# Attention loop: where the bursts of row maxima and their transposition stand among the matmuls

## The chip, the cores and the metric

The kernel runs on one core of a Trainium2 chip. The metric is device time in microseconds (us) of one execution; less is better. The engines in this text are TensorE (PE in the profile; its weight loads are a row of their own, PEld), VectorE (DVE), ScalarE (ACT), GpSimd (POOL) and SyncE (SP, which issues most DMAs). TensorE writes its results to PSUM, from which VectorE and ScalarE read.

## The reference

For 2,048 tokens of width 640, in float32:

```python
xn = layernorm(x)
qkv = xn @ wqkv                       # 32 heads of 20
scores = q @ k^T * 20**-0.5           # keys 0 to 255 positions back
o = softmax(where(mask, scores, -1e9)) @ v
h = gelu(xn @ w_gate) * (xn @ w_up)   # width 1728
out = x + o @ wo + h @ w_down
```

The softmax takes the largest score of each row away before the exponential.

## The kernel before

After a layer norm, the attention loop (`attention`, L789) runs, from about 90 to some 640 us of the profile; the remaining gate and up projections and the down and output projections follow.

**Units and slots.** The loop has 32 units, one for each group of four heads and chunk of 512 tokens (u = 4 * group + chunk). A unit has 14 slots, i = 0 to 13; T = 14 * u + i counts slots through the loop. Twelve steps before it (the ramp) do the first maxima. The order of the instructions on TensorE, VectorE, ScalarE and GpSimd is the order in which the program text issues them (a schedule written by hand), so the slots are no clock: they only say what stands behind what in each engine's queue.

**What a slot issues, in order:**
1. what was deferred to this slot (`tick`), the transposed maxima last;
2. in some slots a burst of maxima (`pull_max(2, T)`: two pairs);
3. in slot 0 the product with V of the unit before (`av_unit`), and then a second burst;
4. in the odd slots 1 to 11 two scores (`exp_piece`): matmuls of keys against queries into a PSUM tile `ps_e` (L545), an exponential on ScalarE from it (L547), and, one slot after the fourth head, masking on GpSimd (`clear`, L558 and L561);
5. `flush`: VectorE work and DMA issues put off with `late`;
6. in slots 9 and 12 the loads of keys and queries for unit u + 3;
7. `pull_fill(RATE / NS)`: about three dense matmuls (L105), a part of the Q, K, V, gate and up projections, in float32 at 128 x 128 weights and 512 columns (320 for V). They fill the loop; what of them is not done in it runs behind it.

**The maxima.** `max_pair(u, i)` does one pair (two of the heads, 128 query rows): small bf16 matmuls on 64 x 64 quarters of the array (L480) into two PSUM tiles `ps_m` out of four, and two reductions with the mask on VectorE (L490). Eight pairs make a unit. A burst is two pairs, so it takes all four PSUM tiles: 8 or 16 small matmuls and four reductions. Bursts run ahead of their unit: those of unit u are issued in slots 4 and 8 of unit u - 2 and twice in slot 0 of unit u - 1. After the eighth pair VectorE negates the maxima (L499, L500), and `max_end` is put down for slot + MXD: a matmul against an identity that transposes them (L507, into a `ps_n` that takes one of the same four PSUM tiles), a copy on ScalarE (L509) and a DMA from ScalarE's queue (L510) into two rows of the unit's query tile `qs`. The score matmuls read these rows, so the maxima are taken away in the matmul itself.

**Dependencies by lag.** What VectorE does with a dense result is followed by ScalarE work a fixed number of slots later, LAG[i] of the slot i in which VectorE's part was issued (`lag`, L214): 3, 5, 4, 4, 4, 4, 3, 3, 4, 3, 2, 1, 1, 1.

Of the kernel before, what the change touches and what calls it, by code (L numbers as in the profile page):

```python
# [30 lines left out]
NS = 14  # L31
RATE = 42.2
V1_SLOT = 158
MXD = 6
KSLOT = 9
LAG = 3, 5, 4, 4, 4, 4, 3, 3, 4, 3, 2, 1, 1, 1
NFA = 6
# [28 lines left out]
def block_kernel(ctx, tc, x, wqk, wv, wgu, wdo, wdl, out):  # L66
# [131 lines left out]
    def at(slot, fn, *a):  # L198
        acts.setdefault(slot, []).append((fn, a))
# [9 lines left out]
    def flush():  # L209
        while lates:  # L210
            fn, a = lates.pop(0)
            fn(*a)
# [108 lines left out]
    def run(*gens):  # L321
        for gen in gens:
            for _ in gen:
                pass
# [121 lines left out]
    def load_stack(u, which=(0, 1)):  # L446
        g, c = divmod(u, NC)
        for m in range(80 * g // 128, (80 * g + 79) // 128 + 1):
            assert all((m + 5 * i, c) in done for i in which), (u, m)

        for i in which:
            dst, src, top, again = ((qs[u % NQ], qd[c], 1, 2), (ks[u % NK], kd[c], 0, 0))[i]
            for j in (0, 2):
                for p, part, n in ((j * 32, top, 2), (j * 32 + 2 * DH, again, 1), (64 - j * 32, 0, 3)):
                    nc.sync.dma_start(dst[p:p + DH * n, j:j + 2].rearrange("p j t -> p (j t)"),
                                      src[g, part:part + n].rearrange("s (d j) t -> (s d) (j t)",
                                                                      j=4)[:, j * C:(j + 2) * C])
# [73 lines left out]
    def exp_piece(u, s):  # L531
        g, c = divmod(u, NC)
        bi, j = divmod(s, 4)
        bank = pieces(c)[bi]
        q = qs[u % NQ]
        if j == 0:
            pts[u, bi] = ap.tile([128, 4, C], F32, name="P", tag="P", bufs=3)
        pt = pts[u, bi]
        lo = min(p[1] for p in bank)
        hi = max(p[1] + p[3] for p in bank)  # L540
        ps = psx.tile([128, C], F32, name="ps_e", tag="ex")
        for kb, col, q0, n in sorted(bank, key=lambda p: p[3]):
            k = ks[(u - (kb < 4 * c)) % NK]
            kc = kb % 4 * 128
            nc.tensor.matmul(ps[:, col:col + n], k[0:QROWS, j, kc:kc + 128], q[0:QROWS, j, q0:q0 + n],  # L545
                             start=True, stop=True)
        nc.scalar.activation(pt[:, j, lo:hi], ps[:, lo:hi], AF.Exp, scale=SCALE)  # L547
        if j == 3:
            defer(1, clear, u, bi)
# [163 lines left out]
    def x_sums(p, k, half):  # L713
        w = C // 2
        a, b = (slice((2 * p + i) * C + half * w, (2 * p + i) * C + half * w + w) for i in (0, 1))
        eh, el = xh.bitcast(F32), xl.bitcast(F32)
        live = {}

        def tile_of(i):
            live[i] = ap.tile([128, w], F32, name="tx", tag="tx")  # L720
            return live[i]

        def pool(o, i, j, op):
            nc.gpsimd.tensor_tensor(out=o, in0=i, in1=j, op=op)

        def store(i):
            t = live[i]
            defer(2, lambda: nc.sync.dma_start(td[p][i][:, k, half * w:half * w + w], t))

        def s1():  # L730
            pool(tile_of(1), eh[:, k, b], eh[:, k, a], OP.subtract)

        def s2():
            pool(live[1], live[1], el[:, k, b], OP.add)

        def s3():
            pool(live[1], live[1], el[:, k, a], OP.subtract)
            store(1)

        def s4():  # L740
            pool(tile_of(2), eh[:, k + 2, b], live[1], OP.subtract)

        def s5():
            pool(live[2], live[2], el[:, k + 2, b], OP.add)
            store(2)

        def s6():
            pool(tile_of(4), eh[:, k + 2, a], live[2], OP.subtract)

        def s7():  # L750
            pool(live[4], live[4], el[:, k + 2, a], OP.add)
            store(4)

        def s8():
            pool(tile_of(3), eh[:, k + 2, b], eh[:, k, b], OP.subtract)

        def s9():
            pool(live[3], live[3], el[:, k + 2, b], OP.add)

        def s10():  # L760
            pool(live[3], live[3], el[:, k, b], OP.subtract)
            store(3)

        return s1, s2, s3, s4, s5, s6, s7, s8, s9, s10
# [6 lines left out]
    def pull_max(n, slot):  # L771
        for _ in range(n):
            x = next(stream, None)
            if x is None:
                return
            max_pair(*x)
            if x[1] == 7:
                at(slot + (MXD if slot >= 0 else 4), max_end, x[0])

    def tick():  # L780
        todo = [y for t in sorted(t for t in acts if t <= now[0]) for y in acts.pop(t)]
        return sorted(todo, key=lambda y: y[0] is max_end)

    def pull_fill(n):
        debt[0] += n
        while debt[0] > 0:
            debt[0] -= next(fill, 1.0)

    def attention():  # L789
        now[0] = -1  # L790
        load_stack(0)
        load_stack(1)
        load_stack(2)
        for i, (p, k, half) in enumerate((p, k, half) for p in range(NC // 2) for k in range(2) for half in range(2)):
            for j, fn in enumerate(x_sums(p, k, half)):
                at(XS0 + XSN * i + 2 * j, fn)
        for i in range(12):
            now[0] = i - 13
            for fn, a in tick():
                fn(*a)  # L800
            if i % 2 == 0:
                pull_max(2, now[0])
            flush()
            pull_fill(2 * RAMP)
        pull_fill(GAP)
        for u in range(NU + 1):
            for i in range(NS):
                T = now[0] = NS * u + i
                for fn, a in tick():
                    fn(*a)  # L810
                if i in (0, 4, 8) or T == 2:
                    pull_max(2, T)
                if i == 0 and u:
                    av_unit(u - 1)
                    flush()
                    pull_max(2, T)
                if i % 2 and i < 12 and u < NU:
                    exp_piece(u, i - 1)
                    if i == 1 and u:
                        pull_fill(1)  # L820
                        debt[0] -= 1
                    exp_piece(u, i)
                flush()
                if u + 3 < NU and i in (KSLOT, 12):
                    load_stack(u + 3, (int(i == KSLOT),))
                pull_fill(RATE / NS)
        while acts:
            now[0] += 1
            for fn, a in tick():
                fn(*a)  # L830
            flush()
        now[0] = None
        run(fill)
        assert not acts

    with tc.manual_schedule(engines=MANUAL | {mybir.EngineType.Pool}):
        attention()
# [575 lines left out]
    for n, (p, k) in enumerate(steps):  # L1413
        i = n % (NQD + 1)
# [71 lines left out]
```

## Time and profile before

| | |
|---|---|
| runs before, median (lowest to highest) | 1067.74 us (1066.36 to 1068.19) |
| the profiled execution | 1067.07 us |
| its span, first to last instruction | 1065.2 us |
| granted TensorE clock, mean | 0.998 |
| maxima: matmuls L480 / reductions L490 | 1472 / 512 |
| scores L545 / exponentials L547 | 704 / 384 |
| transposed maxima L507 | 32 |
| dense matmuls L105, 512 columns | 3 x 430 |

A row of the timeline has the start in us, the time in us, the engine, the line, the operation, what is written and read, the shapes and the count of instructions merged in it. The duration of a matmul is modelled and reaches past the start of the next one; the distance between two starts is what a matmul costs. A row of groups has the busy time and the mean of one in ns, then the idle time before. A row of waits has the engine and line that waited, for whom, the total in us, how often, and the longest.

### The profile page before, as it was taken

To read this page: it belongs to the slowest core of one execution; us is meant where nothing else is said; L and a number is where in the kernel's file an instruction comes from. 1 tells how busy PE (TensorE), PEld (TensorE's weight loads), DVE (VectorE), ACT (ScalarE), POOL (GpSimd) and SP (SyncE) were. 2 spreads that over 40 slices of the span, in tenths; PEclk is the share of its full clock that TensorE was granted. 3 is DMA by queue.
4 is the path that set the end of the run, shared out by engine and by line. 5 is a ranking of instruction groups with operands and counts; after the bars stand their busy time and mean duration, and the time that the engine had idled before them with its cause. 6 is when DMAs were issued, how large, how long until landed. Compare 5 with 4: busy or idle time off the path is not lost.

```text
span 1065.2 us, 25614 instructions
## 1 busy us (share of the span) xinstructions
PE 1052.9 (99%) x9429; PEld 832.7 (78%) x9429; DVE 722.9 (68%) x1985; ACT 531.1 (50%) x1120; POOL 375.6 (35%) x550
## 2 busy tenths in 40 slices
PE   8999999999999999999999999999999999999998
PEld 8877666666678766666666678888888999999998
DVE  7845656565554456666666627787776879888887
ACT  4434665566656565565656565332234543433332
POOL 6021665777764484746556351211100000000000
PEclk9999999999999999999999999999999999999999
DMA  5642344455452244424333215565766873343433
GB/s 196 187 150 75 105 148 131 137 141 176 135 157 81 84 143 122 147 90 139 99 105 123 66 63 199 173 247 204 251 247 247 277 254 129 128 134 103 133 129 105
DMA packets 105190, 158.74 MB, mean 149 GB/s; under 512 B 15420, under 2 KB 60092, under 8 KB 105064
## 3 DMA queue, kind: packets, MB, share of 16 engines
q1 hardware_dynamic: 102680, 150.95, 44.0%
q10 hardware_dynamic: 2384, 6.16, 1.7%
q8 instruction: 74, 1.21, 0.5%
q14 instruction: 52, 0.43, 0.1%
HBM read 101.78 MB, written 54.92 MB: 147 GB/s over the span
## 4 chain that ended last, share of the span: by engine, by line
PE 84%; DVE 5%; POOL 4%; DMA 3%; issue 2%; ACT 2%; SPq 0%; ACTq 0%; DVEq 0%; POOLq 0%
PE ps_d L105 25%; PE ps L1202 19%; PE ps_g L935 16%; PE ps_e L545 7%; PE ps_v L105 6%; PE ps_o L586 5%; PE ps_m L480 4%; PE ps_g L105 1%; POOL pt L247 1%; DVE junk L490 1%; DMA xi<-x 1%; POOL P L561 1%; POOL P L558 1%; DVE ss L1040 1%; DMA hr<-od 1%
## 5 line engine op out<-in xcount | busy, mean ns | idle before, releaser
L490 DVE CUSTOM_DVE_ANT_0 junk<-ps_m,mask 128x320 bf16<-128x320 f32 (+2 forms) x512 | 243.0, 475 | 171.7 <-PE ps_m L480 114.1
L547 ACT ACTIVATE P<-ps_e 128x512 f32<-128x512 f32 (+2 forms) x384 | 199.0, 572 | 106.3 <-PE ps_e L545 102.2
L1202 PE MATMUL ps<-wb,at 128*128 128x320 f32 x999 | 156.1, 309 | 0.3 <-DVE at L1040 0.3
L1202 PEld LDWEIGHTS ps<-wb,at 128*128 128x128 f32 x999 | 148.9, 188 | 0.8 <-DVE at L1040 0.6
L105 PE MATMUL ps_d<-xh,wql 128*128 128x512 f32 x430 | 136.7, 421 | 0.0
L105 PE MATMUL ps_d<-xh,wqh 128*128 128x512 f32 x430 | 135.1, 419 | 0.0
L105 PE MATMUL ps_d<-xl,wqh 128*128 128x512 f32 x430 | 134.8, 418 | 0.0
L545 PE MATMUL ps_e<-qs,ks 124*128 124x128 bf16 (+2 forms) x704 | 118.2, 279 | 0.3
L558 POOL TENSOR_SCALAR_AFFINE_SELECT P<-P 128x512 f32<-128x512 f32 x128 | 82.2, 642 | 101.9 <-ACT P L547 99.5
L545 PEld LDWEIGHTS <-ks 124*128 124x128 bf16 x704 | 48.6, 99 | 61.0 <-issue 48.6
L1202 PE MATMUL ps<-wt,at 128*128 128x320 f32 x552 | 89.2, 310 | 0.8 <-DVE xr L1225 0.8
L105 PEld LDWEIGHTS ps_d<-xl,wqh 128*128 128x128 f32 x430 | 77.4, 189 | 15.4 <-issue 3.4
L105 PEld LDWEIGHTS ps_d<-xh,wql 128*128 128x128 f32 x430 | 77.0, 189 | 15.7 <-issue 3.6
L105 PEld LDWEIGHTS ps_d<-xh,wqh 128*128 128x128 f32 x430 | 76.7, 189 | 15.5 <-issue 3.1
L1202 PEld LDWEIGHTS ps<-wt,at 128*128 128x128 f32 x552 | 82.9, 188 | 1.3 <-DVE xr L1225 1.0
L561 POOL TENSOR_SCALAR_AFFINE_SELECT P<-P 128x512 f32<-128x512 f32 x112 | 70.8, 642 | 35.4 <-ACT P L547 35.4
L1156 ACT ACTIVATE at<-ss 128x512 fp32r<-128x512 f32 x59 | 37.3, 633 | 88.5 <-DVE ss L1040 88.5
L586 PE MATMUL ps_o<-P,v 64*32 64x320 f32 (+4 forms) x2816 | 75.9, 348 | 0.9 <-POOL P L561 0.6
L247 POOL TENSOR_TENSOR pt<-r,pt 128x512 bf16<-128x512 f32 x40 | 46.5, 1164 | 77.1 <-ACT pt L246 73.7
L586 PEld LDWEIGHTS ps_o<-P,v 64*32 64x32 f32 x2816 | 48.5, 106 | 26.6 <-POOL P L558 3.4
L480 PE MATMUL ps_m<-ks,qs 60*64 60x320 bf16 (+3 forms) x1472 | 63.3, 260 | 2.6 <-DVE xl L192 1.1
L480 PEld LDWEIGHTS <-qs 60*64 60x64 bf16 x1472 | 28.3, 105 | 42.1 <-issue 36.7
(195 smaller groups left out, 1754.0 us busy)
## 6 DMA issues: line engine op xcount, KB each, us to landing
hr<-hd SPq DMA_DIRECT2D x104, 128.0 KB
hd<-he SPq DMA_DIRECT2D x50, 256.0 KB
wr<-wgu SPq DMA_DIRECT2D x27, 320.0 KB
qs<-qd SPq DMA_DIRECT2D x64, 120.0 KB
ks<-kd SPq DMA_DIRECT2D x64, 120.0 KB
xi<-x SPq DMA_DIRECT2D x16, 320.0 KB
qs<-qd SPq DMA_DIRECT2D x64, 80.0 KB
ks<-kd SPq DMA_DIRECT2D x64, 80.0 KB
```

The lines of the kernel that those rows point to most:

```text
L105: nc.tensor.matmul(ps, a(k), b(k), start=n == 0, stop=n == 3 * nk - 1)
L247: nc.gpsimd.tensor_tensor(out=pt[:, l, :], in0=r, in1=pt[:, 1, :], op=OP.subtract)
L480: nc.tensor.matmul(ps[64 * h:64 * h + 64, col:col + w], q[rows, j, q0:q0 + 64], ks_, start=True, stop=True, tile_position=(64 * r, 64 * h))
L490: nc.vector.tensor_tensor_reduce(out=junk[:, 0:n], in0=ps[:, 320 - n:320], in1=mask[:, 320 - n:320], scale=1.0, scalar=NEG, op0=OP.add, op ...
L545: nc.tensor.matmul(ps[:, col:col + n], k[0:QROWS, j, kc:kc + 128], q[0:QROWS, j, q0:q0 + n], start=True, stop=True)
L547: nc.scalar.activation(pt[:, j, lo:hi], ps[:, lo:hi], AF.Exp, scale=SCALE)
L558: nc.gpsimd.affine_select(out=a, in_=a, pattern=[[0, 4], [1, 128]], compare_op=OP.is_ge, fill=0.0, base=0, channel_multiplier=-1)
L561: nc.gpsimd.affine_select(out=a, in_=a, pattern=[[0, 4], [-1, 128]], compare_op=OP.is_ge, fill=0.0, base=-1, channel_multiplier=1)
L586: nc.tensor.matmul(os[r][32 * j:32 * j + 32, qa:qb], v[rows, w0_:w0_ + 32], pt[rows, j, col + qa - q0:col + qb - q0], start=r not in begun ...
L935: nc.tensor.matmul(ps, i, j, start=first and n == 0, stop=n == len(work) - 1, skip_group_check=True)
L1156: nc.scalar.activation(hi[:, 3:7], s, AF.Copy)
L1202: nc.tensor.matmul(ps[bank][:, 0:HD], *work[bank][j], start=bank not in begun, stop=final[p, bank] == n and j == len(work[bank]) - 1, skip ...
```

## The change

Three numbers of the slot plan. The bursts of slots 4 and 8 are issued in slots 5 and 9, which have scores: there the burst stands ahead of the two scores and behind the three dense matmuls of the slot before. In unit 0 the extra burst of slot 2 goes to slot 3. The delay of the transposed maxima is 7 slots instead of 6, so for most units they go from slot 6 to slot 7, ahead of that slot's scores. The lags stay as they are.

```diff
-MXD = 6
+MXD = 7
 KSLOT = 9
 LAG = 3, 5, 4, 4, 4, 4, 3, 3, 4, 3, 2, 1, 1, 1
...
                 for fn, a in tick():
                     fn(*a)
-                if i in (0, 4, 8) or T == 2:
+                if i in (0, 5, 9) or T == 3:
                     pull_max(2, T)
                 if i == 0 and u:
                     av_unit(u - 1)
```

## The prediction

> **What bounds the kernel now.** I read the page first (engine sums, clock, chain), then who waited for whom on TensorE inside the attention loop, then the starts of single matmuls around one burst.
>
> ```profile
> span 1065.2 us, 25614 instructions
> PE 1052.9 (99%) x9429; PEld 832.7 (78%) x9429; DVE 722.9 (68%) x1985; ACT 531.1 (50%) x1120; POOL 375.6 (35%) x550
> PEclk9999999999999999999999999999999999999999
> PE 84%; DVE 5%; POOL 4%; DMA 3%; issue 2%; ACT 2%; SPq 0%; ACTq 0%; DVEq 0%; POOLq 0%
> ```
>
> TensorE is busy for 99% of the span at full clock and has 84% of the chain. "Busy" says little about waste, because the ends of matmuls are modelled; the starts are what I use. The waits of TensorE on other engines between 100 and 620 us, all of them:
>
> ```profile
> PE ps_m L480 <- DVE mx L490: 0.7, 2, 0.4
> PE ps_o L586 <- POOL P L561: 0.6, 1, 0.6
> ```
>
> 1.3 us in 520. So in the loop TensorE's own order of instructions sets the time: what an order saves on TensorE comes off the end (the dense work that fills the loop runs on behind it), unless another engine becomes late.
>
> **The seams of TensorE.** One slot-4 burst among 512-column dense matmuls, then the end of a slot-8 burst, each row a start time and a modelled duration:
>
> ```profile
> 457.31 0.39 PE L105 MATMUL ps_d<-xl,wqh 128*128 128x512 f32 x1
> 457.54 0.40 PE L105 MATMUL ps_d<-xl,wqh 128*128 128x512 f32 x1
> 457.87 0.47 PE L480 MATMUL ps_m<-ks,qs 60*64 60x256 bf16 x16
> 458.27 0.50 PE L105 MATMUL ps_d<-xl,wqh 128*128 128x512 f32 x1
> 458.60 0.39 PE L105 MATMUL ps_d<-xl,wqh 128*128 128x512 f32 x1
> 458.83 0.40 PE L105 MATMUL ps_d<-xl,wqh 128*128 128x512 f32 x1
> ...
> 462.27 0.47 PE L480 MATMUL ps_m<-ks,qs 60*64 60x320 bf16 x8
> 462.67 0.50 PE L105 MATMUL ps_d<-xh,wql 128*128 128x512 f32 x1
> 463.01 0.63 PE L105 MATMUL ps_d<-xl,wqh 128*128 128x512 f32 x2
> ```
>
> Dense to dense is 0.23 us (457.31 to 457.54, 458.60 to 458.83). Into the burst it is 0.33 (457.54 to 457.87): 0.10 is lost. The first dense matmul behind the burst takes 0.33 until the next one (458.27 to 458.60), and 0.34 at the other burst (462.67 to 463.01): another 0.10 lost, the dense weights that could not be loaded while the burst ran. That second loss is what the change touches. Now the transposed maxima and a pair of scores:
>
> ```profile
> 459.99 0.40 PE L105 MATMUL ps_d<-xh,wqh 128*128 128x512 f32 x1
> 460.23 0.23 PE L507 MATMUL ps_n<-identb,nm 128*128 128x128 bf16 x1
> 460.27 0.47 PE L105 MATMUL ps_d<-xh,wqh 128*128 128x512 f32 x1
> 460.58 0.39 PE L105 MATMUL ps_d<-xh,wqh 128*128 128x512 f32 x1
> 460.81 0.40 PE L105 MATMUL ps_d<-xh,wql 128*128 128x512 f32 x1
> 461.05 0.28 PE L545 MATMUL ps_e<-qs,ks 124*128 124x256 bf16 x1
> ...
> 463.24 0.40 PE L105 MATMUL ps_d<-xl,wqh 128*128 128x512 f32 x1
> 463.48 0.23 PE L545 MATMUL ps_e<-qs,ks 124*128 124x128 bf16 x1
> 463.55 0.55 PE L545 MATMUL ps_e<-qs,ks 124*128 124x384 bf16 x3
> 463.79 0.54 PE L105 MATMUL ps_d<-xl,wqh 128*128 128x512 f32 x1
> 464.17 0.63 PE L105 MATMUL ps_d<-xl,wqh 128*128 128x512 f32 x2
> ```
>
> Dense to score is 0.24 (463.24 to 463.48, 460.81 to 461.05): only 0.01 lost. The four score matmuls (1,024 columns) and the dense one behind them take 463.48 to 464.17 = 0.69; less a dense 0.23 that is 0.46, and 1,024 columns at the dense rate of 0.23/512 are 0.46. So scores have practically no seam. The transposed maxima do: 460.23 to 460.58 less 0.23 is 0.12 for 128 columns, which at that rate are 0.06; the dense weights are longer than this short matmul can cover. A 128-column score with another score behind it takes 0.07 (463.48 to 463.55).
>
> **The change part by part.**
> *Bursts of slots 4 and 8 to slots 5 and 9, ahead of the scores.* Nothing is added or removed: 8 or 16 small matmuls with their weight loads on TensorE and four reductions with their reads on VectorE move past one slot's three dense matmuls. No DMA, SyncE or GpSimd instruction belongs to a burst. The scores, their exponentials and the dense matmuls keep their order among themselves. The stream has 256 pairs; 12 go in the ramp and 8 in unit 0, so at 8 a unit slots 4 and 8 carry bursts in units 0 to 29: 60 bursts. Each keeps the 0.10 on entry. Behind it now stands a score, so the 0.10 of exposed dense weights becomes the exposed weights of a score, x, and the 0.01 from dense to score goes. Saving: 0.11 - x.
>
> x is nowhere in this trace, as no score stands behind a burst. Ends: 0.10, if a score's weights take as long as dense ones (saving 0.01 each, 0.6 us in all); 0, if they load within what the burst's end costs anyway (0.11 each, 6.6 us). The nearest rows are the weight loads themselves:
>
> ```profile
> L105 PEld LDWEIGHTS ps_d<-xl,wqh 128*128 128x128 f32 x430 | 77.4, 189 | 15.4 <-issue 3.4
> L545 PEld LDWEIGHTS <-ks 124*128 124x128 bf16 x704 | 48.6, 99 | 61.0 <-issue 48.6
> ```
>
> 99 ns against 189, so about half: x = 0.05. The 0.07 from one score to the next says the same, since a load of 0.10 would not fit in it. I take 0.06 a burst: 60 x 0.06 = 3.6 us.
>
> [...]
>
> *Transposed maxima from slot 6 to slot 7.* With the delay at 7 and the last pair still pulled in slot 0, they stand in slot 7 behind three more dense matmuls and directly ahead of scores. 30 of 32 gain (units 2 to 31; that of unit 0 is in the ramp, that of unit 1 goes from slot 8 to slot 10, which has no scores). Each costs 0.07 as a score before a score does, instead of 0.12, and one step from dense to score, 0.01, goes: 0.06 x 30 = 1.8 us. Ends: 0.01 x 30 = 0.3 if a score behind it is no better off than a dense matmul, and (0.12 - 0.06 + 0.01) x 30 = 2.1 if only its columns remain.
>
> The ScalarE copy moves with it, and so does the DMA issue, which now comes behind two exponentials:
>
> ```profile
> L509 ACT ACTIVATE mr<-ps_n x32: 247/266/268, 84.8 to 613.2; 32x128 bf16<-32x128 f32 x32
> L510 ACTq DMA_DIRECT2D qs<-mr x32: 620/622/1238, 85.1 to 613.5; - x32
> 461.94 1.08 ACT L547 ACTIVATE P<-ps_e 128x512 f32<-128x512 f32 x2 [0.70 <-PE ps_e L545]
> 472.33 1.09 ACT L547 ACTIVATE P<-ps_e 128x512 f32<-128x512 f32 x2 [0.47 <-PE ps_e L545]
> ```
>
> ScalarE waits 0.70 us for scores in that slot today; the copy's 0.27 fits inside. The row of maxima is needed by the next unit's first scores, near 472, and its DMA would be issued near 463.0 instead of 461.3: some 9 us ahead. I cost this at nothing.
>
> *The unit-0 burst from slot 2 to 3:* one more burst ahead of scores, 0.06, against the lone transposition in slot 10. Nothing.
>
> *What the later bursts do to VectorE.* After the slot-8 burst:
>
> ```profile
> 465.00 0.08 DVE L490 DVE_READ_ACCUMULATOR2_ANT mx<- 128x1 f32 x1
> 466.07 0.69 DVE L646 SCALAR_TENSOR_TENSOR he<-he,gs 128x512 f32<-128x512 f32 x1 [0.99 <-ACT he L641]
> 467.92 0.47 PE L480 MATMUL ps_m<-ks,qs 60*64 60x256 bf16 x16
> DVE r L261 <- POOL pt L247: 14.3, 6, 3.1
> ACT ob L592 <- PE ps_o L586: 68.7, 25, 4.0
> ```
>
> The reductions end 2.8 us after the burst begins (462.27 to 465.08). The burst comes three dense matmuls later, 0.7, so they end near 465.8: before the next operation starts at 466.07, and 2.1 us before the burst that reuses their PSUM tiles (467.92). The cover is that 2.1 us; if it is gone, TensorE stands at that burst for what is missing. The operations deferred by fixed numbers of slots (the lags at slots 9 and 10) reach ScalarE with some 0.7 us less spare; a short wait there falls into the time that ScalarE stands idle ahead of the AV copies (68.7 us over 25 times, up to 4.0) and I cost it at nothing.
>
> **Sum.** 3.6 + 1.8 = 5.4 us. The profiled execution took 1067.07 us (span 1065.2), so 1061.7 by it; it lies 0.7 under the median of the runs, 1067.74, which gives 1062.3. By the ends: 0.6 + 0.3 = 0.9 us (1066.8) to 6.6 + 2.1 = 8.7 us (1059.0).
>
> **The rivals.**
> *A score's weights cost behind a burst what dense ones cost.* Then 0.9 us are left: 1066.8; a difference under 0.2%, 2.1 us, is about what a measurement of this kernel cannot tell from none. For it: the loss of 0.10 could be a fixed latency of the switch and not a load's length; no row shows otherwise behind a burst. Against it: the load rows of 99 and 189 ns and the pitch of 0.07. [...]
>
> *VectorE gets late and the PSUM tiles of the maxima with it (slower).* The place is the slot-0 burst. VectorE once stood 3.1 us for GpSimd (the row above, 6 waits); if such a stand comes between the moved burst and slot 0, the 2.1 us of cover turn into 1.0 us of TensorE waiting. It decides the sign from about 5.4 us in all, so with a wait in at least 6 units; in 10 units it gives 1062.3 + 10 = 1072. For it: cover shrinks by 0.7 in every unit, and the deferred operations of slots 9 and 10 now queue behind the reductions. Against it: two waits of 0.7 us in all today, and VectorE idle 0.99 us right behind the burst.
>
> *The whole seam goes.* If the score's weights load during the end of the burst, x is 0 and the time 1059. For it: only that TensorE loads ahead elsewhere; against it: dense weights do not do so behind a burst.
>
> That the change doesn't do what it says is hardly one: the order on TensorE is written by hand and followed.
>
> **How the numbers follow.** The saving of about half an exposed load (2.2 to 7 us): 0.73, of it 0.05 towards the whole seam. No difference in the load: 0.13. VectorE late: 0.12, mostly with a loss, some of it only eating the gain. The rest, 0.02, is an unnamed loss. Faster by over 0.2%: 0.75 with the mild cases of a late VectorE; within: 0.14; slower: 0.11. The range runs from 1059.0, the end of the sum, to 1066.8, the first rival; the forecast's own is 1060.5 to 1065.5.
>
> **What would show it.** Right: a slot-5 or slot-9 burst is followed by a score as soon as it is now by a dense matmul (457.87 to 458.27 here), and the score after that comes only some 0.05 later than the columns ask; a first dense matmul of 0.33 is left only behind slot 0's bursts; the transposed maxima are followed by a score after about 0.07. Wrong: a score delayed by 0.10 behind a burst, new rows of TensorE waiting for the reductions, or of ScalarE's copies waiting for VectorE, or a span that moves while the seams do not.

## The result, and the profile after

| | before | after | ratio, 95% interval |
|---|---|---|---|
| first measurement | 1067.77 us | 1060.58 us | 0.993 (0.9908 to 0.9952) |
| second one, on another occasion | 1068.47 us | 1058.09 us | 0.9908 (0.9893 to 0.9922) |

The change makes the kernel 7 to 10 us faster; 5.4 us had been forecast (1062.3 us). The page of the changed kernel, its span, engines and chain:

```profile
span 1057.7 us, 25616 instructions
PE 1042.1 (99%) x9429; PEld 837.7 (79%) x9429; DVE 722.2 (68%) x1985; ACT 532.1 (50%) x1120; POOL 376.0 (36%) x550
PE 82%; DVE 6%; POOL 4%; issue 3%; DMA 3%; ACT 2%; SPq 1%; ACTq 0%; DVEq 0%; POOLq 0%
```

The same counts on every engine, the same share of busy TensorE, a shorter span. Where the time went shows in the two ends of the loop: the first start of a maxima matmul (L480) and the first start of the stage behind (L935). By line, a row has the durations of one in ns (least, median, most), then the first and last start; the first two rows are of the kernel before, the other two of the changed one:

```profile
L480 PE MATMUL ps_m<-ks,qs x1472: 186/268/321, 61.4 to 607.0; 60*64 60x320 bf16 x64, 60*64 60x256 bf16 x55, 60*64 60x128 bf16 x48, 60*64 60x64 bf16 x16
L935 PE MATMUL ps_g<-xh,wqh x126: 389/389/390, 651.4 to 822.1; 128*128 128x512 f32 x126
```

```profile
L480 PE MATMUL ps_m<-ks,qs x1472: 186/268/321, 59.8 to 596.9; 60*64 60x320 bf16 x64, 60*64 60x256 bf16 x55, 60*64 60x128 bf16 x48, 60*64 60x64 bf16 x16
L935 PE MATMUL ps_g<-xh,wqh x126: 389/389/389, 641.2 to 811.9; 128*128 128x512 f32 x126
```

From 61.4 to 651.4 the loop took 590.0 us; from 59.8 to 641.2 it takes 581.4. So 8.6 us left the loop. The start in the changed profile is 1.6 us earlier, and the part behind the loop 2.7 us longer. Of both, the clock explains a part. Windows of both kernels (the columns are the stretch, its length, busy time of PE, PEld, DVE, ACT and POOL with counts, then the granted clock, the DMA share and GB/s), before first:

```profile
0.00:60.00 60.00, 56.23 (x369) 51.17 (x370) 42.31 (x117) 25.29 (x77) 20.24 (x39) 0.97 0.52 172
860.00:870.00 10.00, 10.00 (x71) 10.00 (x69) 5.10 (x9) 3.27 (x4) 0.00 (x0) 1.00 0.87 320
```

```profile
0.00:60.00 60.00, 54.94 (x386) 49.61 (x386) 43.33 (x119) 26.60 (x80) 20.27 (x39) 1.00 0.53 177
860.00:870.00 10.00, 8.13 (x46) 7.87 (x45) 8.95 (x19) 3.92 (x9) 0.00 (x0) 0.83 0.59 198
```

Each profile has one short stretch of lower clock, worth 60 x 0.03 = 1.8 and 10 x 0.17 = 1.7 us of full clock, but in a different place: ahead of the loop before, behind the loop after. It is no part of the change; the loop is the cleaner measure.

**The seams after.** One slot of transposed maxima and a slot-9 burst with its scores, starts of single matmuls of the changed kernel:

```profile
470.18 0.23 PE L507 MATMUL ps_n<-identb,nm 128*128 128x128 bf16 x1
470.25 0.60 PE L545 MATMUL ps_e<-qs,ks 124*128 124x256 bf16 x4
...
471.85 0.40 PE L105 MATMUL ps_d<-xh,wql 128*128 128x512 f32 x1
472.18 0.47 PE L480 MATMUL ps_m<-ks,qs 60*64 60x320 bf16 x8
472.58 0.61 PE L545 MATMUL ps_e<-qs,ks 124*128 124x128 bf16 x4
472.64 0.38 PE L545 MATMUL ps_e<-qs,ks 124*128 124x384 bf16 x2
```

The transposition is followed by a score after 0.07 us. Into the burst it is 0.33 still (471.85 to 472.18), and from the burst's first matmul to what follows 0.40 (472.18 to 472.58), as from 462.27 to 462.67 before. Of these 0.40 us, 0.24 pass from the start of the last four small matmuls to what follows (472.34 to 472.58, and 462.43 to 462.67 before); their 320 columns at the dense rate of 0.23/512 are 0.144. In three decimals the 0.24 is 0.238 (median of 31 such bursts with a score behind) and 0.236 (of 64 with a dense matmul before), so by this estimate about 0.09 is a seam that a score pays like a dense matmul; behind bursts that end on 192 columns it is 0.208 and 0.206 from the same start. But behind that, the 128-column score is followed by the next after 0.06 to 0.07 us (472.58 to 472.64; the row of four scores at 472.58 includes the two of the row below), no more than between scores behind a dense matmul (463.48 to 463.55 before). The same holds throughout: of the 98 bursts that a dense matmul followed, 61 now have a score behind them, and the 30 of these that begin with 128 columns are followed after 0.065 to 0.067 us, the 30 with 256 columns after 0.12. No cost of a score's weights behind a burst shows beyond the 0.09: x is 0.00, not 0.05, and the delay of some 0.05 that the prediction named as a sign did not show. The waits of TensorE on other engines between 100 and 620 us are few as before, 2.2 us in all instead of 1.3:

```profile
PE ps_m L480 <- DVE mx L490: 1.0, 3, 0.3
PE ps_o L586 <- POOL P L561: 0.8, 2, 0.6
PE ps_e L545 <- ACT P L547: 0.4, 1, 0.4
```

### The profile page after: what moved, and what is told of

Same layout as the page of the kernel before. It is cut to its first block, busy times and chain, and to the rows that moved or that the text cites. A ratio compares the mean times of both kernels' runs of the same rounds, so it can differ in the third digit from the quotient of the medians.

```text
span 1057.7 us, 25616 instructions
## 1 busy us (share of the span) xinstructions
PE 1042.1 (99%) x9429; PEld 837.7 (79%) x9429; DVE 722.2 (68%) x1985; ACT 532.1 (50%) x1120; POOL 376.0 (36%) x550
## 4 chain that ended last, share of the span: by engine, by line
PE 82%; DVE 6%; POOL 4%; issue 3%; DMA 3%; ACT 2%; SPq 1%; ACTq 0%; DVEq 0%; POOLq 0%
PE ps_d L105 24%; PE ps L1202 17%; PE ps_g L935 16%; PE ps_e L545 7%; PE ps_v L105 6%; PE ps_o L586 5%; PE ps_m L480 4%; POOL pt L247 1%; PE ps_g L105 1%; DVE junk L490 1%; DVE ss L1040 1%; POOL P L561 1%; POOL P L558 1%; DMA hr<-hd 1%; DMA stg<-wtd 1%
## 5 line engine op out<-in xcount | busy, mean ns | idle before, releaser
L105 PE MATMUL ps_d<-xh,wql 128*128 128x512 f32 x430 | 131.4, 415 | 0.0
L105 PE MATMUL ps_d<-xl,wqh 128*128 128x512 f32 x430 | 130.2, 412 | 0.0
L105 PE MATMUL ps_d<-xh,wqh 128*128 128x512 f32 x430 | 130.0, 413 | 0.0
L480 PE MATMUL ps_m<-ks,qs 60*64 60x320 bf16 (+3 forms) x1472 | 62.6, 260 | 3.0 <-DVE mx L490 1.2
L480 PEld LDWEIGHTS <-qs 60*64 60x64 bf16 x1472 | 28.2, 105 | 41.9 <-issue 37.2
```

What stands on the lines that cost most here:

```text
L105: nc.tensor.matmul(ps, a(k), b(k), start=n == 0, stop=n == 3 * nk - 1)
L480: nc.tensor.matmul(ps[64 * h:64 * h + 64, col:col + w], q[rows, j, q0:q0 + 64], ks_, start=True, stop=True, tile_position=(64 * r, 64 * h))
```

## The experiments

Two theories were set against each other. By the *seams*, a burst followed by a score saves what a dense matmul behind it loses, and the transposition saves when a score follows. By the *spacing*, what helps is that the bursts stand 5, 4 and 5 slots apart instead of 4, 4 and 6, which relieves VectorE and the PSUM tiles. "Loop" is again the distance from the first L480 to the first matmul of the stage behind, in the run's profile; where the clock was lower for a moment within it, the second number has that taken off. That stretch, of the changed kernel on the second occasion, looked like this (bursts_only, maxima_only, earlier and later_apart have the same 0.86 there, 12 x 0.14 = 1.7 us):

```profile
58.00:70.00 12.00, 10.70 (x65) 8.05 (x63) 6.38 (x18) 4.81 (x10) 1.39 (x2) 0.86 0.57 170
```

| kernel | time, us | ratio to before, 95% interval | loop, us | against 590.0 |
|---|---|---|---|---|
| changed kernel, second occasion | 1058.09 | 0.9908 (0.9893 to 0.9922) | 582.7, 581.0 | -9.0 |
| bursts_only | 1060.16 | 0.9931 (0.9913 to 0.9948) | 584.6, 582.9 | -7.1 |
| maxima_only | 1068.19 | 0.9991 (0.9976 to 1.0005) | 590.2, 588.5 | -1.5 |
| dense_between | 1066.34 | 0.9984 (0.9973 to 0.9996) | 587.3 | -2.7 |
| behind_scores | 1066.73 | 0.9977 (0.9962 to 0.9993) | 587.7 | -2.3 |
| earlier | 1060.90 | 0.9929 (0.9909 to 0.9948) | 584.4, 582.7 | -7.3 |
| later_apart | 1070.08 | 1.0013 (0.9997 to 1.0029) | 591.9, 590.2 | +0.2 |
| extra_bf16 | 1070.58 | 1.0028 (1.0014 to 1.0042) | 591.0 | +1.0 |

The kernel before took 1068.4 to 1068.5 us beside these.

**The changed kernel again.**

> The changed kernel once more, for its time on the chip of the next three. Both theories: about 7 us under the kernel before, near 1060.6 us; a loop (first maxima to last dense matmul of the loop) about 8.5 us shorter.

The loop was 9.0 us shorter, the time 10.4, with an interval of 8.3 to 11.4 that takes in the 9.0. Both theories stand.

**Bursts alone.** Of the change only the places of the bursts:

```diff
 # after.py
-MXD = 7
+MXD = 6
```

> Bursts in slots 5, 9 (and 3 of unit 0) ahead of the scores, the transposed maxima left in slot 6. Theory of the seams (a score behind a burst has no exposed weight load, a dense matmul has 0.105): 61 x 0.11 = 6.7 us of the loop's 8.5 stay, the time is 1.8 above the changed kernel, near 1062. Theory of the spacing (bursts 5, 4, 5 slots apart instead of 4, 4, 6 relieve VectorE and the PSUM tiles): all of it stays, near 1060.6.

8.3 us under the kernel before (1060.16 against 1068.47), 7.1 in the loop, where the seams ask for 6.7. The time is 2.1 above the changed kernel's of that occasion. The spacing theory, by which all of the gain stays, is the worse one here, though 2 us are close to what the intervals can tell.

**Transposed maxima alone.**

```diff
 # before.py
-MXD = 6
+MXD = 7
```

> Only the transposed maxima go to slot 7, the bursts stay in slots 4 and 8. Theory of the seams: 30 x 0.06 = 1.8 us faster than the kernel before, near 1066. Theory of the spacing: no change, 1067.8.

1.5 us in the loop, as the seams have it (1.8); the time is 0.3 us under the kernel before with an interval that reaches from a gain of 2.6 to a loss of 0.5 (0.24% and 0.05% of 1068), so the timing alone shows nothing and only the trace tells. 7.1 and 1.5 make 8.6, the whole of the first profile's gain: the parts add.

**One dense matmul between burst and scores.** The bursts keep their slots, and only the neighbour changes:

```diff
 # after.py
                 if i in (0, 5, 9) or T == 3:
                     pull_max(2, T)
+                    if i:
+                        pull_fill(1)
+                        debt[0] -= 1
```

> As the changed kernel, but one of the dense matmuls of the slot stands between the burst and the scores of slots 5 and 9. The bursts keep their slots, VectorE its order. Theory of the seams: each burst has the exposed dense weights back, 60 x 0.11 = 6.6 us, so near 1067 and the first dense matmul behind those bursts at 0.33 again. Theory of the spacing: still near 1060.6.

```profile
461.88 0.47 PE L480 MATMUL ps_m<-ks,qs 60*64 60x320 bf16 x8
462.28 0.50 PE L105 MATMUL ps_d<-xl,wqh 128*128 128x512 f32 x1
462.62 0.61 PE L545 MATMUL ps_e<-qs,ks 124*128 124x128 bf16 x4
```

Here the time from the dense matmul behind the burst to the next is back at 0.34 (462.28 to 462.62), and of the gain 2.1 us are left (1066.34 against 1068.47), what the maxima alone are to give. This tells the theories apart: same slots, same order on VectorE, no gain from the bursts.

**Bursts behind the scores.** In the same slots, next to the same scores, but on their other side:

```diff
 # after.py
-                if i in (0, 5, 9) or T == 3:
+                if i == 0:
                     pull_max(2, T)
...
                     exp_piece(u, i)
+                if i in (5, 9) or T == 3:
+                    pull_max(2, T)
                 flush()
```

> As the changed kernel, but the bursts of slots 5 and 9 stand behind that slot's two scores instead of ahead. Theory of the seams: dense weights are exposed behind them again, only the transposed maxima's 1.8 us is left: about 2 us under the kernel before. Theory of the spacing, or of any nearness to scores: still about 7 to 10 us under it.

2.3 us in the loop, 1.7 in the time. The dense matmul behind the burst is again followed after 0.34 (480.77 to 481.11 in that trace). Nearness to scores is nothing by itself; it is what follows the burst.

**Earlier, with the same neighbours.**

```diff
 # after.py
-MXD = 7
+MXD = 5
...
-                if i in (0, 5, 9) or T == 3:
+                if i in (0, 3, 7) or T == 5:
```

> Bursts ahead of the scores of slots 3 and 7 (unit 0 has one more in slot 5), the transposed maxima ahead of those of slot 5: the same neighbours, but bursts 3, 4, 7 slots apart. Theory of the seams: the same 8.5 us less in the loop, less any wait of TensorE for VectorE's reductions at slot 3, where the four PSUM tiles of slot 0 have only some 2.6 us to come free. Theory of the spacing: slower than the kernel before, whose gaps are 4, 4, 6.

7.5 us under the kernel before (1060.90 against 1068.44) with the least even gaps of all, 3, 4 and 7 slots. The spacing theory falls. The loop is 1.3 us longer than the changed kernel's 581.4. The waits of TensorE between 60 and 660 us, less 1.3 at the start that both profiles have, are 3.5 us instead of 2.4, 0.5 of the difference for VectorE's reductions, which the expectation had named, and the rest for masks and exponentials.

**Later, without the neighbours.**

```diff
 # after.py
-                if i in (0, 5, 9) or T == 3:
+                if i in (0, 6, 10) or T == 4:
```

> Bursts in slots 6 and 10 (and 4 of unit 0), between dense matmuls on both sides, the transposed maxima next to scores in slot 7: later by two slots, without the neighbours. Theory of the seams: only the transposed maxima's 1.8 us, about 2 us under the kernel before. Theory of the spacing: gaps of 6, 4, 4, no better than 4, 4, 6. A late VectorE would show here as waits of TensorE at slot 0's first burst, more than in the changed kernel.

The time is not told from that of before, where the maxima's 1.8 should have been left. The waits of TensorE between 100 and 620 us:

```profile
PE ps_o L586 <- POOL P L561: 2.6, 3, 1.3
PE ps_m L480 <- DVE mx L490: 1.6, 5, 0.4
PE ps_e L545 <- ACT P L547: 0.2, 1, 0.2
```

4.4 us instead of 1.3: TensorE waits 3.1 us more for VectorE's reductions and GpSimd's masks, where the loop lacks 1.7 to 2.0 us of the maxima's gain. That these waits are what took the gain is argued from their size; no run separates it. By one slot, as in the change, the waits rose by 0.9.

**A bf16 matmul behind the burst that is no score.** The prediction took half of a dense matmul's loss for a score, and the trace says none. Is that the scores, or any bf16 weights?

```diff
 # before.py
-        pss = [psm.tile([128, 320], F32, name="ps_m", tag="mx") for _ in range(2)]
+        pss = [psm.tile([128, C], F32, name="ps_m", tag="mx") for _ in range(2)]
...
         quarters(lambda lo, hi: (k, max(0, -lo), max(0, lo), hi))
+        if i in (1, 3) and now[0] >= 0:
+            nc.tensor.matmul(pss[1][:, 384:512], identb, identb, start=True, stop=True)
```

> The kernel before (bursts in slots 4 and 8) with one more bf16 matmul right behind each of these 60 bursts, ahead of the dense ones: identity weights of 128 x 128 against 128 columns, into columns of the PSUM tile that nobody reads. It is the first matmul of the whole array behind a burst, like a score, but without the scores. If bf16 weights load unseen behind a burst (x = 0), from it to the second dense matmul it is 0.35 us, as from a transposition today (460.23 to 460.58), in place of 0.33 from the first dense matmul to the second: 60 x 0.02, about 1 us slower in all. If x is 0.05 as predicted, 0.40 and about 4 us slower; if a bf16 load were exposed like a dense one, 0.45 and about 7 us slower.

```profile
155.23 0.47 PE L480 MATMUL ps_m<-ks,qs 60*64 60x320 bf16 x8
155.63 0.23 PE L489 MATMUL ps_m<-identb 128*128 128x128 bf16 x1
155.66 0.94 PE L105 MATMUL ps_d<-xh,wql 128*128 128x512 f32 x3
155.98 0.40 PE L105 MATMUL ps_d<-xh,wql 128*128 128x512 f32 x1
```

From the extra matmul to the second dense one it is 0.35 (155.63 to 155.98), as behind a transposition among dense matmuls, and the loop is 1.0 us longer, as worked out for x = 0. The time rose by 2.1 (1070.58 against 1068.51), of which the other 1.1 are not accounted for. So here a full 128 x 128 bf16 load behind a burst costs nothing that shows beyond the 0.09, scores or not.

## Why the prediction was right, point by point

- *TensorE's order sets the time in the loop, so that a seam saved comes off the end.* Right: nothing but order changed in bursts_only, dense_between and behind_scores, and their gains lie up to 6.6 us apart.
- *The loss of 0.10 behind a burst is exposed dense weights.* Right in the place: it is gone when a score follows, and back at 0.34 with one dense matmul between. That it is no fixed cost of the switch is shown by extra_bf16, where a bf16 matmul follows without the loss. That it is the load of the float32 weights, and not something else in a float32 matmul behind a burst, is argued: no run separates the two.
- *x = 0.05, by the ratio of the two rows of weight loads.* This term was mis-sized: x is 0.00. With it the sum is 61 x 0.11 + 1.8 = 8.5 us, and the loops measured 8.6 and 9.0. It was luck that the first median, 1060.58, still lay within the forecast's own 1060.5 to 1065.5; the second, 1058.09, lies below even the 1059.0 at the end of the sum. The rival "the whole seam goes", held at 0.05 with 1059 us, had the size right, and the times lie on both sides of it. Its reason, that the load runs during the end of the burst, is not shown: the row of the first load starts within 0.01 us of its matmul's, at 472.57 for the score and at 462.67 for the dense matmul. The step that failed was to scale the part that shows with the length of the load. What shows beyond the 0.09 was 0.10 for a load of 189 ns and nothing for one of 99 ns, which is no proportion. Their difference, 90 ns, is near the 0.10, so the rows would also fit if the 0.09 that both pay were the first part of the load; no run tests this.
- *The rival by which a score's weights cost what dense ones do.* Wrong: by it a score behind a burst loses the 0.10 that a dense matmul loses there, and the 30 scores of 128 columns are followed after 0.065 to 0.067 us, as between scores behind a dense matmul (463.48 to 463.55 before). It left 0.9 us of gain; the loops were 8.6 and 9.0 us shorter.
- *The transposed maxima, 1.8 us.* Right in the trace: 1.5 in the loop and 0.07 to the score behind; too small for the timing of that kernel alone.
- *Each burst keeps the 0.10 on entry.* Right: it is 0.33 into the burst in the changed kernel too (471.85 to 472.18), where two dense starts lie 0.23 apart. What these 0.10 consist of, no run shows.
- *VectorE's cover of 2.1 us holds.* Right for a shift of one slot: waits of TensorE rose from 1.3 to 2.2 us. The rival was no phantom, as with a shift of two slots they were 4.4 us and the maxima's gain was gone.

What stays open: whether a bf16 load lies within the 0.09 that score and dense matmul both pay behind a burst or is too short to show, and why float32 weights then show 0.10 more; where the 1.1 us of extra_bf16 outside the loop come from; and what the length of the part behind the loop, which varies between profiles by up to 3 us (413.8 before, 416.9 in maxima_only), depends on beside the clock.

## What to carry to other kernels

Where one engine is saturated, read the starts of its instructions, not their durations, and price each kind of neighbour: into, out of, and between. Here a burst of small tiled matmuls cost 0.10 us where a dense matmul stood ahead of it, about 0.09 (the estimate above) towards the score or dense matmul behind it, and 0.10 more where that one was dense; what follows should be the matmul that loses least there, here a bf16 one instead of a float32 one. That took a move of each burst past three dense matmuls and no new instruction. Where the price of a new neighbour isn't in the trace, both ends of its range belong into the forecast, as the true one was an end.

## What the runs showed of the hardware that was not expected

- Behind a burst of 64 x 64 tiles a matmul with bf16 weights was followed as soon as without a burst: after 0.065 to 0.067 us for the 30 scores of 124 rows and 128 columns (0.07 from 463.48 to 463.55 before), and after 0.35 by the second dense matmul for the identity of 128 rows (155.63 to 155.98, and 460.23 to 460.58 before). One with float32 weights and 512 columns was followed after 0.33 to 0.34 us instead of 0.23.
- The clock fell for a few microseconds once or twice in a profile, at places that differ between profiles (0.97 over the first 60 us before, there 0.50 from 14 to 16 and 0.65 from 16 to 18; 0.86 between 58 and 70 on the second occasion; 0.83 between 860 and 870 after), worth about 1.7 us of full clock each; in dense_between and behind_scores it was 0.94 over the first 58 us, worth twice that. At a gain of 0.7% that is a quarter of the effect, and it can lie within the stretch that is compared.
